# State-space scan with a feed-forward layer on one core: the written-out issue order of the first four units re-sorted

## The chip, the cores and the metric

The kernel runs on one core of one Trainium2 chip. The metric is the device time of the kernel in microseconds (us). Lower is better.

## The reference

The reference computes a chunked state-space scan, and feeds its result into a two-layer network with a squared ReLU. Cut to what matters:

```
# x [4,8,768,32], a [4,8,768], B and C [4,8,768,16]; chunk = 32 positions
for c in range(768 // 32):
    cum   = cumsum(log(clip(a_c, 1e-6, 1)))
    M     = (C_c @ B_c.T) * exp(cum_i - cum_j) * causal      # per batch and head
    y_c   = M @ x_c + (C_c @ state) * exp(cum_i)
    state = exp(sum(la)) * state + sum_j B_j x_j exp(cum_last - cum_j)
t   = y.transpose(0, 2, 1, 3).reshape(3072, 256)
out = (maximum(t @ w_in, 0) ** 2) @ w_out                    # 256 -> 2048 -> 256
```

## The kernel before

**Units.** The 3072 tokens are cut into 12 units of 256 tokens: one of four batches, one of three thirds of the sequence. The first thirds of the four batches come first, so that the scan's state reaches a unit four units later. The scan works on a whole unit at once. The products P of the decays are folded into C, and their inverses (`Pinv`) into x, so that what is left of M is a plain product C·B under a 0/1 mask.

**Steps of a unit k.** Each step is a short word in a list, with the unit's number behind it.
- `ldC`, `ldB`, `ldx`: loads of float32 C, B, x, issued on SP's queue. `pc` (`prep_c`, L167): C scaled by P into a bf16 tile `jt`, in two instructions. `pb` (`prep_b`, L175 or L179): B cast into `jt`. `px` (`prep_x`, L187): x scaled by `Pinv`, into `xs`.
- `tr`: `jt` turned around into `bct`. For units 0 to 3 TensorE does it (L205), and `tc` copies the result out (L218 on ScalarE, L220 on VectorE); from unit 4 on a transposing transfer of SP's queue does it (L196).
- `mt`: the 16 score matmuls C·B (L235) into PSUM banks 0 to 3. `mk`: VectorE masks one bank straight from PSUM (L244). Instead of that, `sc` copies a bank to SBUF on ScalarE (L249), and `ms` masks the copy (L253) on VectorE or GpSimd.
- `u`: the state's update (L260, 16 matmuls, `xs` by `jt`). `ina`, `inb`: the two halves of the masked scores times `xs` (L260, 32 matmuls together). `sf`: the first state scaled (L388, tile `Sd`). `ca`: C times the state (L260, 2 matmuls `bct` by `Sd`). `t`: the unit's result copied into `T` (L218, L220, L327). `us`, `za`, `sa` and the like carry the state on.
- `a0` to `a7` for unit 0, `b0` to `b7` for unit 1 and so on: one eighth of the first layer, 4 matmuls of `w_in_b` (L451) and a ReLU on ScalarE (L472). `qa0`: VectorE squares it (L478). `A0` to `A7`: one eighth of the second layer (4 matmuls, L451 again), accumulated in one bank; the last one is followed by a copy to `osb` (L500) and the store (L501).
- `id`: filler matmuls on constants (L552). `wi0` to `wi3`, `wo0` to `wo3`: the four pieces of w_in and w_out, issued by GpSimd (L148, L152).
- `gB3` and the like: a small memset (L143) that keeps a load back until the engine named gets to it. `afC`, `afK`, `afS`: small copies on GpSimd (L668 to L676) that hold GpSimd's following work back until a C, a prefix scan or a state is there.
- `ac1`, `p2`, `pp1`, `pd`, `iv`: decay products of the second and last third. `p2` is 16 matmuls (L519, L523, L632); the last four of them need `pick_p`, which `pp1` makes on ScalarE (L620). `pd` copies the result, and `iv` makes `Pinv` of it. `jz2` (L593) clears the third `jt` tile.

**What sets the order.** Nothing is planned at run time. One string `ORDER` is split at blanks, and each word issues its step; each engine works off its own instructions in that order, and waits on semaphores. `:a`, `:v`, `:p`, `:s` behind a word name the engine or queue (ScalarE, VectorE, GpSimd, SP), `:va` one for each of two instructions, `@3` a PSUM bank.

Of the kernel before, what the change touches and what calls it, by code (L numbers as in the profile page):

```python
# [30 lines left out]
def kernel(  # L31
# [14 lines left out]
    NH, S, D, N = 8, 768, 32, 16  # L46
    NU = 12
    ORDER = """
        fa1:a jz0:v ef jz1:p id3:512 ti fa0:s la0:s id4:512 pi eb ldB0:s ac0:v ldC0:a sk0 ku sp la1:a pbh0:p hd id1:256
        pc0:v pbl0:v mb:a id2:512 trC0 ps iv:8:16 tcC0:1:a tcC0:0:v trB0 la2:s tcB0:2:v pk id1:512 iv1:0:8 id1:512  # L50
        ldx0:s mt0 wi0 la3:s px0:v ldC1:s su id2:512 ldB1:s wi1 ldx1:s u0:67 mk0 fq mk0 gC2:v mk0 ac1:v pc1:p sc0 pb1:a
        id2:512 tr1 id4:512 tc1:1:a tc1:0:a to ms0:p sf0 sk1 wo0 afK px1:p wi2 mt1 ina0 inb0 ca0 pp1:a mk1 mk1 t0:aa sc1
        us0 mk1 fr p2@4 a0 ldC2:s a1 u1::6 ina1 ms1:v wo1 wi3 jz2:p pc2 inb1 sf1 ca1 pd t1:va us1 a3@0 qa1 ldB2:s qa0
        a2@1 wo2 b0@2 qa3 qb0 b1@3 qb1 b2@4 b3@5 A0 A1 B0 pb2:p B1 tr2 zb0 qb3 gB3:v ldx2:s ldB3:s ldC3:s ldx3:s b4 a4
        iv:32:64 zb1 tc2:1:v qa2 tc2:0:v b5 sb1 sb0 qb4 a5 qb2 qa4 mt2 sc2 B3 iv:16:32 px2 pc3 wo3 mk2 mk2 sc2 A3 A2
        ms2:v ms2:v qa5 a6 b6 pb3:a B2 a7 qb5 qa6 b7 u2 ina2 inb2 sf2 afS2 px3 ld4 A4 tr3 ca2 tc3:1:v t2:aa B4 us2 B5
        tc3:0:v u3:45 pc4 mt3 A5 us3 sc3 c5 qb7 qb6 mk3 za3 pb4 ldC5:s ldB5:s c3 qa7 c4 qc5 c0 qc3 px4 tr4 ldx5:s pb5
        pc5 sa3 c1 c6 ldC6:s tr5 ldB6:s ldx6:s qc4 qc0 A6 px5 pq A7 wm c2 B6 c7 C0 ms3:v mk3 qc6 mk3 qc7 afC2 pc6 B7 C3
        C6 C4 qc1 bk rg4 C1 qc2 d1 d0 za4 sa4 pb6 mk4 mk4 d3 mk4 C5 d4 qd0 d2 mk4 px6 tr6 ld7 C2 C7 qd1 qd2 qd3 zb3 rg5
        sb3 D0 mk5 za5 sa5 D1 mk5 d5 qd4 D2 pc7 pb7 d6 qd5 d7 qd6 D3 zb2 e0 qd7 mk5 e1 qe0 sb2 D4 mk5 D5 tr7 ld8 e2 qe1  # L60
        D6 e3 qe2 ml px7 rg6 e4 D7 qe3 za6 sa6 zb6 mk6 e5 qe4 sb6 e6 qe5 e7 qe6 iv:64:96 mk6 E0 E1 E2 E3 ldC9:s ldB9:s
        px8 mk6 f0 qe7 E4 f1 qf0 pc8 E5 pb8 tr8 ldx9:s E6 mk6 f2 qf1 f3 qf2 E7 rg7 mk7 F0 f4 qf3 za7 F1 F2 f5 qf4 f6 qf5
        f7 qf6 g0 qf7 zb7 sa7 sb7 mk7 F3 mk7 F4 pc9 pb9 tr9 px9 ld10 g1 qg0 F5 mk7 g2 qg1 zb4 sb4 F6 g3 qg2 F7 rg8 za8
        zb8 sa8 sb8 g4 qg3 G0 mk8 g5 qg4 G1 mk8 g6 qg5 G2 g7 qg6 G3 mk8 h0 qg7 G4 pc10 pb10 tr10 px10 ld11 h1 qh0 G5 mk8
        zb5 sb5 h2 qh1 G6 h3 qh2 G7 rg9 za9 zb9 sa9 sb9 h4 qh3 H0 mk9 h5 qh4 H1 mk9 h6 qh5 H2 h7 qh6 H3 mk9 i0 qh7 H4
        pc11 pb11 tr11 px11 i1 qi0 H5 mk9 i2 qi1 H6 i3 qi2 H7 rg10 za10 zb10 sa10 sb10 i4 qi3 I0 mk10 i5 qi4 I1 mk10 i6
        qi5 I2 i7 qi6 I3 mk10 j0 qi7 I4 j1 qj0 I5 mk10 j2 qj1 I6 j3 qj2 I7 rg11 za11 zb11 sa11 sb11 j4 qj3 J0 mk11 j5
        qj4 J1 mk11 j6 qj5 J2 j7 qj6 J3 mk11 k0 qj7 J4 k1 qk0 J5 mk11 k2 qk1 J6 k3 qk2 J7 rg12 k4 qk3 K0 k5 qk4 K1 k6
        qk5 K2 k7 qk6 K3 l0 qk7 K4 l1 ql0 K5 l2 ql1 K6 l3 ql2 K7 l4 ql3 L0 l5 ql4 L1 l6 ql5 L2 l7 ql6 L3 ql7"""
    LATE = 6  # L70
    WIN = [(0, 2), (2, 4), (4, 6), (6, 8)]
    WOUT = [(0, 2), (2, 4), (4, 6), (6, 8)]
# [807 lines left out]
```

## Time and profile before

| | |
|---|---|
| times of three runs | 113.91, 113.81, 113.87 us; median 113.87 us |
| the profiled execution | 113.92 us, with a span of 112.2 us and 3692 instructions |
| mean granted TensorE clock | 1.0 |
| TensorE busy | 106.8 us (95%) in 1453 matmuls |
| VectorE, ScalarE, GpSimd busy | 83.0, 76.8, 50.9 us |
| moved by DMA | 13.44 MB, 120 GB/s on average |

The span runs from the first to the last instruction of the profiled execution; 1.72 us of its time lie around it. The times named in the text are microseconds from the start of the span. In a row of the timeline the first number is the start and the second the time from the first to the end of the last of the instructions put together there; the bracket behind it is the idle time before it and what ended it.

### The profile page before, as it was taken

How to read it: one execution, taken by the hardware profiler on the slowest of the kernel's cores; microseconds unless marked ns; L12 is line 12 of the kernel's file. 1: busy time of each engine (PE TensorE's matmuls, PEld its weight loads, DVE VectorE, ACT ScalarE, POOL GpSimd, SP SyncE). 2: the span in 40 equal slices, each digit the busy share in tenths (PEclk: the TensorE clock that was granted, in tenths of full speed). 3: DMA queues.
4: the chain of work that ended last, by engine and by line, in shares of the span. 5: the costliest groups of instructions: out<-in, count | busy, mean ns of one | idle time of the engine just before them, and what ended most of it. 6: DMA issues, size and time to landing. Idle time of an engine off the chain costs nothing.

```text
span 112.2 us, 3692 instructions
## 1 busy us (share of the span) xinstructions
PE 106.8 (95%) x1453; PEld 92.0 (82%) x1454; DVE 83.0 (74%) x189; ACT 76.8 (68%) x159; POOL 50.9 (45%) x98
## 2 busy tenths in 40 slices
PE   6988999998999999999999999999999999999990
PEld 2434799886997989989989989889899899899980
DVE  1688858996793988979977989679589398355440
ACT  1745994885894776685677676877876867867840
POOL 7589973259676564378038653573160020000000
PEclk9999999999999999999999999999999999999999
DMA  1999999979989799987994997799680020020203
GB/s 38 198 186 164 211 193 201 156 148 188 148 171 97 92 284 64 110 188 72 103 179 48 138 217 74 99 196 98 129 211 0 6 96 0 29 70 0 93 0 94
DMA packets 67281, 13.44 MB, mean 120 GB/s; under 512 B 63104, under 2 KB 65984, under 8 KB 67264
## 3 DMA queue, kind: packets, MB, share of 16 engines
q1 hardware_dynamic: 64320, 10.88, 59.3%
q0 software_dynamic: 1664, 2.10, 11.4%
q10 hardware_dynamic: 1280, 0.23, 1.1%
q8 instruction: 11, 0.18, 0.7%
q14 instruction: 6, 0.05, 0.1%
HBM read 10.58 MB, written 3.15 MB: 122 GB/s over the span
## 4 chain that ended last, share of the span: by engine, by line
PE 77%; DMA 8%; ACT 4%; SPq 3%; POOL 2%; issue 2%; DVE 1%; ACTq 0%; POOLq 0%
PE pp L451 66%; PE pp L260 6%; DMA C_nat<-in_C_dram 5%; DMA B_nat<-in_B_dram 3%; ACT hb L472 2%; PE pp L229 2%; SPq L134 1%; SPq L654 1%; PE pp L235 1%; POOL jt L167 1%; POOL xs L187 1%; ACT bct L218 1%; PE pp L205 0%; DVE Sd L388 0%; DVE h L478 0%
## 5 line engine op out<-in xcount | busy, mean ns | idle before, releaser
L472 ACT ACTIVATE hb<-pp 128x512 bf16<-128x512 f32 x96 | 54.5, 602 | 21.8 <-PE pp L451 20.2
L451 PE MATMUL pp<-w_out_b,h 128*128 128x256 bf16 (+1 forms) x400 | 53.8, 268 | 0.0
L451 PE MATMUL pp<-T,w_in_b 128*128 128x256 bf16 x384 | 53.3, 273 | 0.0
L478 DVE TENSOR_TENSOR h<-hb 128x512 bf16<-128x512 bf16 x96 | 44.5, 485 | 11.4 <-ACT hb L472 11.2
L451 PEld LDWEIGHTS <-w_in_b 128*128 128x128 bf16 x384 | 41.4, 114 | 1.8 <-issue 1.1
L451 PEld LDWEIGHTS <-h 128*128 128x128 bf16 x400 | 37.6, 98 | 4.5 <-issue 1.0
L244 DVE TENSOR_TENSOR mts<-pp,mask 128x512 bf16<-128x512 f32 x43 | 28.5, 678 | 1.3 <-PE pp L235 0.7
L187 POOL TENSOR_TENSOR xs<-x_nat,Pinv 128x256 bf16<-128x256 f32 (+1 forms) x19 | 13.4, 722 | 14.8 <-DMA x_nat<-in_x_dram 6.7
L376 POOL TENSOR_TENSOR Sd<-z,Pquad 128x256 bf16<-128x256 f32 x16 | 11.0, 698 | 10.0 <-DVE z L360 6.7
L167 POOL TENSOR_TENSOR jt<-C_nat,P_sb 128x128 bf16<-128x128 f32 x22 | 10.0, 472 | 8.9 <-DMA C_nat<-in_C_dram 8.8
L360 DVE SCALAR_TENSOR_TENSOR z<-z,Ptot,us 128x64 f32<-128x64 f32 x8 | 3.3, 407 | 7.4 <-ACT us L344 5.0
L552 PE MATMUL pp<-const-bfloat16-1.0 128*128 128x512 bf16 (+1 forms) x19 | 6.5, 464 | 1.0 <-PEq L864 0.8
L500 ACT COPY osb<-pp 128x512 f32<-128x512 f32 x11 | 6.4, 583 | 0.4 <-PE pp L451 0.4
L175 POOL CAST jt<-B_nat 128x256 bf16<-128x256 f32 x9 | 4.6, 511 | 3.9 <-DMA B_nat<-in_B_dram 2.9
L260 PE MATMUL pp<-mts,xs 64*32 64x128 bf16 (+1 forms) x288 | 5.4, 219 | 0.0
L260 PE MATMUL pp<-bct,Sd 128*128 128x128 bf16 x40 | 4.2, 220 | 0.2 <-DVE Sd L388 0.2
L552 PEld LDWEIGHTS <-const-bfloat16-1.0 128*128 128x128 bf16 x20 | 1.8, 111 | 2.6 <-issue 2.2
L260 PEld LDWEIGHTS <-xs 64*32 64x32 bf16 (+1 forms) x288 | 3.6, 93 | 0.4 <-issue 0.2
L260 PEld LDWEIGHTS <-Sd 128*128 128x128 bf16 x40 | 3.0, 98 | 0.7 <-DVE Sd L388 0.4
L260 PEld LDWEIGHTS <-jt 64*32 64x32 bf16 (+1 forms) x128 | 1.6, 90 | 2.2 <-issue 1.2
L249 ACT CAST sc<-pp 128x512 bf16<-128x512 f32 x5 | 2.9, 607 | 0.6 <-PE pp L235 0.5
L148 POOL DMA_DIRECT2D w_in_b<-in_moe_w_in_dram x4 | 3.1, 776 | 0.3 <-issue 0.3
(77 smaller groups left out, 58.3 us busy)
## 6 DMA issues: line engine op xcount, KB each, us to landing
out_dram<-osb SPq DMA_DIRECT2D x11, 256.0 KB, 3.0
x_nat<-in_x_dram SPq DMA_DIRECT2D x6, 256.0 KB, 4.9
w_in_b<-in_moe_w_in_dram POOLq DMA_DIRECT2D x4, 256.0 KB, 5.6
w_out_b<-in_moe_w_out_dram POOLq DMA_DIRECT2D x4, 256.0 KB, 6.4
B_nat<-in_B_dram SPq DMA_DIRECT2D x6, 128.0 KB, 4.5
C_nat<-in_C_dram SPq DMA_DIRECT2D x12, 64.0 KB, 3.9
B_nat<-in_B_dram SPq DMA_DIRECT2D x12, 64.0 KB, 3.0
x_nat<-in_x_dram SPq DMA_DIRECT2D x6, 128.0 KB, 3.3
```

The costliest lines, as they stand in the source:

```text
L167: eng.tensor_tensor(out=_fap(jt[k % 3], 128 + 144 * g, [[384, 2], [32, 4], [1, 16]]), in0=_fap(loaded[k]["C"], 128 * g, [[16, 2], [32, 4], ...
L175: fn(out=_fap(jt[k % 3], 0, [[384, 2], [16, 2], [32, 4], [1, 16]]), in_=_fap(loaded[k]["B"], 0, [[16, 2], [128, 2], [32, 4], [1, 16]]))
L187: eng.tensor_tensor(out=_fap(xs, 256 * r, [[256, 2 // n], [32, 8], [1, 32]]), in0=_fap(loaded[k]["x"], 32 * r, [[32, 2 // n], [64, 8], [1, ...
L244: nc.vector.tensor_tensor(out=live[k]["mts"][:, q].rearrange("p r g i -> p (r g i)"), in0=pp[:, q, :], in1=mask1 if k >= LATE else mask, o ...
L260: nc.tensor.matmul(dst, w, v, start=bool(need), stop=False, skip_group_check=True, **({} if pos is None else {"tile_position": pos}))
L360: nc.vector.scalar_tensor_tensor(out=z, in0=prev[0], scalar=Ptot[:, total(1, b, j - 1):total(1, b, j - 1) + 1], in1=us, op0=ALU.mult, op1= ...
L376: nc.gpsimd.tensor_tensor(out=_fap(S_d, 0, [[128, 2], [32, 4], [1, 32]]), in0=_fap(z, 0, [[32, 2], [0, 4], [1, 32]]), in1=_fap(Pquad, 4 * ...
L451: nc.tensor.matmul(dst, w(0, 128), v, skip_group_check=True, **flags)
L472: nc.scalar.activation(out=hb.rearrange("p i t -> p (i t)"), in_=pp[:, h, :], func=AF.Relu)
L478: nc.vector.tensor_tensor(out=h2, in0=hb, in1=hb, op=ALU.mult)
L500: nc.scalar.copy(out=osb, in_=pp[:, 6 if blk == 1 else 7, :])
L552: nc.tensor.matmul(pp[:, h, 0:int(cols)], ones_b[:, 0:128], ones_b[:, 0:int(cols)] if dep is None else dep, start=True, stop=True, skip_gr ...
```

## The change

The first 234 of the list's 561 words are re-sorted; the 327 from `bk rg4 C1` on, which is the fifth unit's feed-forward work and everything behind it, stay as they are. No function is changed. The parts:

- Engines: `px0` goes from VectorE to GpSimd and stands behind `pc1`; `pbl0` and a copy of unit 0's turned C go from VectorE to ScalarE; one copy of `tc1` from ScalarE to VectorE; `jz2` from GpSimd to VectorE; both halves of `t1` onto VectorE; `pb2` from GpSimd and `pb3` from ScalarE to VectorE. Of unit 2 one ScalarE copy with its mask (`sc2`, `ms2`) becomes a direct mask (`mk2`).
- Start: `u0`, `ina0` and `inb0` stand around unit 1's transposes and scores; `pp1` stands behind `t0`, not ahead of it; one more filler stands ahead of `ca1`, others are moved. 20 filler matmuls there are in both.
- Weights: the fourth piece of w_in (`wi3`) is issued behind `pc2`, which was the other way round.
- Middle: `B3` stands ahead of `mt2`, `b5` behind `B2`, `mt3` ahead of `u3`.
- Loads: B of unit 5 stands ahead of its C; C of unit 6 and x of unit 5 stand ahead of the two transposing transfers of units 4 and 5; B and x of unit 6 stand behind the first store.

```
-  … ldx0:s mt0 wi0 la3:s px0:v ldC1:s su … wi1 ldx1:s u0:67 mk0 fq mk0 gC2:v mk0 ac1:v pc1:p sc0 pb1:a id2:512 tr1
-  id4:512 tc1:1:a tc1:0:a to ms0:p sf0 sk1 wo0 afK px1:p wi2 mt1 ina0 inb0 ca0 pp1:a mk1 mk1 t0:aa sc1
-  us0 mk1 fr p2@4 a0 ldC2:s a1 u1::6 ina1 ms1:v wo1 wi3 jz2:p pc2 inb1 sf1 ca1 pd t1:va us1 a3@0 …
-  b3@5 A0 A1 B0 pb2:p B1 tr2 zb0 qb3 gB3:v ldx2:s ldB3:s ldC3:s ldx3:s b4 a4 … b5 … mt2 sc2 B3 … A3 A2 …
-  … A4 tr3 ca2 tc3:1:v t2:aa B4 us2 B5 tc3:0:v u3:45 pc4 mt3 A5 …
-  ldC5:s ldB5:s … tr4 ldx5:s pb5 pc5 sa3 c1 c6 ldC6:s tr5 ldB6:s ldx6:s qc4 …
+  … ldx0:s iv1:0:8 wi0 mt0 la3:s ldC1:s su … ldx1:s sc0 mk0 wi1 mk0 pc1:p pb1:a px0:p fq id4:512 ms0:p tr1@01 tc1:1:a
+  mk0 gC2:v u0:67:5 ina0 tc1:0:v to id1:512 mt1 sf0 inb0 ac1:v wo0 sk1 afK ca0 px1:p t0:aa pp1:a mk1 mk1 wi2
+  mk1 us0 fr sc1 p2@4 a0@0 a1@1 ms1:v wo1 u1::6 sf1 pd ldC2:s ina1 inb1 jz2:v pc2 wi3 id1:512 ca1 t1:vv us1 a3@0 …
+  b3@5 b2 qb1 A0 ldx2:s A1 B0 B1 zb0 qb3 pb2:v tr2 gB3:v ldB3:s ldC3:s ldx3:s b4 … B3 mt2 mk2 … A3 … A2 … b5 …
+  ldB5:s qa6 ca2 B5 tc3:1:v t2:aa B4 us2 pb4 tc3:0:v mt3 u3:45 us3 ldC5:s … ldC6:s ldx5:s … tr4 … tr5 …
+  … C0 ldB6:s ldx6:s C3 …
```

In the rows below a tile's name has its unit and a running number at the end; all lines of the changed file are 20 lower, since the string is shorter (L147 is L167 of the profile, and so on).

On GpSimd, from the scaling of C for unit 1 to that for unit 2, before:

```order
L167 TENSOR_TENSOR jt1_111<-C_nat1_207,P_sb_106 128x2x4x16 x2
L253 TENSOR_TENSOR mts0_202<-sc0_3_242,mask_90 128x512
L152 DMA w_out_b0_117<-in_moe_w_out_dram 128x1024
L672 COPY gate_cp_266<-cp128_103 128x1
L187 TENSOR_TENSOR xs1_268<-x_nat1_215,Pinv_107 128x512
L148 DMA w_in_b2_115<-in_moe_w_in_dram 128x2x512
L152 DMA w_out_b1_118<-in_moe_w_out_dram 128x1024
L148 DMA w_in_b3_116<-in_moe_w_in_dram 128x2x512
L593 MEMSET jt2_112 128x768
L167 TENSOR_TENSOR jt2_112<-C_nat2_236,P_sb_106 128x2x4x16 x2
```

The same stretch of GpSimd after:

```order
L147 TENSOR_TENSOR jt1_111<-C_nat1_205,P_sb_106 128x2x4x16 x2
L167 TENSOR_TENSOR xs0_222<-x_nat0_183,Pinv_107 128x512
L233 TENSOR_TENSOR mts0_203<-sc0_0_214,mask_90 128x512
L132 DMA w_out_b0_117<-in_moe_w_out_dram 128x1024
L652 COPY gate_cp_314<-cp128_103 128x1
L167 TENSOR_TENSOR xs1_318<-x_nat1_212,Pinv_107 128x512
L128 DMA w_in_b2_115<-in_moe_w_in_dram 128x2x512
L132 DMA w_out_b1_118<-in_moe_w_out_dram 128x1024
L147 TENSOR_TENSOR jt2_112<-C_nat2_239,P_sb_106 128x2x4x16 x2
L128 DMA w_in_b3_116<-in_moe_w_in_dram 128x2x512
```

The scaling of unit 0's x has come in ahead of the mask of its score copy, the clearing of the third `jt` tile has gone, and the fourth piece of w_in is issued behind unit 2's C.

On ScalarE, from the cast of unit 1's B to the first ReLU, before:

```order
L175 CAST jt1_111<-B_nat1_212 128x2x2x4x16
L218 COPY bct1_247<-pp_121 128x384 x2
L609 COPY Ptot_108<-pp_121 128x8
L620 ACTIVATE pick_p128_105<-pick_95,cp128_103 128x16
L218 CAST T0_325<-pp_121 128x4x64 x2
L249 CAST sc1_2_328<-pp_121 128x512
L341 COPY us0_330<-pp_121 128x128
L472 ACTIVATE hb0_0_345<-pp_121 128x512
```

The same stretch of ScalarE after:

```order
L155 CAST jt1_111<-B_nat1_210 128x2x2x4x16
L198 COPY bct1_230<-pp_121 128x384
L589 COPY Ptot_108<-pp_121 128x8
L198 CAST T0_320<-pp_121 128x4x64 x2
L600 ACTIVATE pick_p128_105<-pick_95,cp128_103 128x16
L324 COPY us0_328<-pp_121 128x64 x2
L229 CAST sc1_3_331<-pp_121 128x512
L452 ACTIVATE hb0_0_345<-pp_121 128x512
```

The activation that makes `pick_p` now follows the two copies of unit 0's result, and one of the two copies of unit 1's transposes is gone to VectorE.

On SP's queue, from the x of unit 4 to the first store, before:

```order
L134 DMA x_nat4_683<-in_x_dram 128x8x64
L134 DMA C_nat5_768<-in_C_dram 128x8x32
L134 DMA B_nat5_770<-in_B_dram 128x8x32
L196 DMA_TRANSPOSE bct4_799<-jt1_111 128x6x128
L134 DMA x_nat5_801<-in_x_dram 128x8x64
L129 DMA C_nat6_820<-in_C_dram 128x8x16 x2
L196 DMA_TRANSPOSE bct5_823<-jt2_112 128x6x128
L129 DMA B_nat6_825<-in_B_dram 128x8x16 x2
L129 DMA x_nat6_828<-in_x_dram 128x8x32 x2
L501 DMA out_0_dram<-osb0_847 128x512
```

The same stretch of SP after:

```order
L114 DMA x_nat4_676<-in_x_dram 128x8x64
L114 DMA B_nat5_693<-in_B_dram 128x8x32
L114 DMA C_nat5_750<-in_C_dram 128x8x32
L109 DMA C_nat6_760<-in_C_dram 128x8x16 x2
L114 DMA x_nat5_763<-in_x_dram 128x8x64
L176 DMA_TRANSPOSE bct4_790<-jt1_111 128x6x128
L176 DMA_TRANSPOSE bct5_825<-jt2_112 128x6x128
L481 DMA out_0_dram<-osb0_846 128x512
L109 DMA B_nat6_865<-in_B_dram 128x8x16 x2
L109 DMA x_nat6_868<-in_x_dram 128x8x32 x2
```

The transposing transfer of unit 4 has three loads ahead of it that stood behind it, and the first store overtakes four loads.

More of the change, by code (lines that the diff above doesn't have):

```diff
@@ L48 @@
     ORDER = """
[L49 to L68, printed above, removed]
@@ L69 @@
-        qk5 K2 k7 qk6 K3 l0 qk7 K4 l1 ql0 K5 l2 ql1 K6 l3 ql2 K7 l4 ql3 L0 l5 ql4 L1 l6 ql5 L2 l7 ql6 L3 ql7"""
+        jz0:v jz1:p fa1:a ef id3:512 fa0:s ac0:v ti pi la0:s id4:512 eb ldB0:s ku ldC0:a sk0 sp la1:a mb:a id1:512 pbh0:p pc0:v id2:512 trC0 ps iv:8:16 hd pbl0:a tcC0:1:a tcC0:0:a la2:s trB0 tcB0:2:v pk id1:512 id1:512 ldx0:s iv1:0:8 wi0 mt0 la3:s ldC1:s su id2:512 ldB1:s ldx1:s sc0 mk0 wi1 mk0 pc1:p pb1:a px0:p fq id4:512 ms0:p tr1@01 tc1:1:a mk0 gC2:v u0:67:5 ina0 tc1:0:v to id1:512 mt1 sf0 inb0 ac1:v wo0 sk1 afK ca0 px1:p t0:aa pp1:a mk1 mk1 wi2 mk1 us0 fr sc1 p2@4 a0@0 a1@1 ms1:v wo1 u1::6 sf1 pd ldC2:s ina1 inb1 jz2:v pc2 wi3 id1:512 ca1 t1:vv us1 a3@0 qa0 a2@1 ldB2:s b0@2 wo2 qa3 b1@3 qa1 qb0 b3@5 b2 qb1 A0 ldx2:s A1 B0 B1 zb0 qb3 pb2:v tr2 gB3:v ldB3:s ldC3:s ldx3:s b4 iv:32:64 zb1 tc2:1:v qb2 tc2:0:v sb1 qa2 a4 qb4 a5 qa4 sb0 B3 mt2 mk2 iv:16:32 px2:p pc3:p sc2 ms2:v wo3 mk2 mk2 qa5 A3 pb3:v A2 a6 b6@1 B2 b5 qb5 a7 b7@3 u2 ina2 inb2 sf2 ld4 afS2 px3:p A4 tr3 ldB5:s qa6 ca2 B5 tc3:1:v t2:aa B4 us2 pb4 tc3:0:v mt3 u3:45 us3 ldC5:s sc3 A5 pc4 ldC6:s ldx5:s c5 qb6 za3 qa7 mk3 c4 qb7 c3 tr4 qc5 px4 c0 pb5 qc3 pc5 c1 pq sa3 qc0 c6 tr5 qc4 c7 px5 A6 A7 c2 B6 afC2 C0 ldB6:s ldx6:s C3 ms3:v mk3 qc6 mk3 wm qc7 C4 qc1 pc6 C6 B7 bk rg4 C1 qc2 d1 d0 za4 sa4 pb6 mk4 mk4 d3 mk4 C5 d4 qd0 d2 mk4 px6 tr6 ld7 C2 C7 qd1 qd2 qd3 zb3 rg5 sb3 D0 mk5 za5 sa5 D1 mk5 d5 qd4 D2 pc7 pb7 d6 qd5 d7 qd6 D3 zb2 e0 qd7 mk5 e1 qe0 sb2 D4 mk5 D5 tr7 ld8 e2 qe1 D6 e3 qe2 ml px7 rg6 e4 D7 qe3 za6 sa6 zb6 mk6 e5 qe4 sb6 e6 qe5 e7 qe6 iv:64:96 mk6 E0 E1 E2 E3 ldC9:s ldB9:s px8 mk6 f0 qe7 E4 f1 qf0 pc8 E5 pb8 tr8 ldx9:s E6 mk6 f2 qf1 f3 qf2 E7 rg7 mk7 F0 f4 qf3 za7 F1 F2 f5 qf4 f6 qf5 f7 qf6 g0 qf7 zb7 sa7 sb7 mk7 F3 mk7 F4 pc9 pb9 tr9 px9 ld10 g1 qg0 F5 mk7 g2 qg1 zb4 sb4 F6 g3 qg2 F7 rg8 za8 zb8 sa8 sb8 g4 qg3 G0 mk8 g5 qg4 G1 mk8 g6 qg5 G2 g7 qg6 G3 mk8 h0 qg7 G4 pc10 pb10 tr10 px10 ld11 h1 qh0 G5 mk8 zb5 sb5 h2 qh1 G6 h3 qh2 G7 rg9 za9 zb9 sa9 sb9 h4 qh3 H0 mk9 h5 qh4 H1 mk9 h6 qh5 H2 h7 qh6 H3 mk9 i0 qh7 H4 pc11 pb11 tr11 px11 i1 qi0 H5 mk9 i2 qi1 H6 i3 qi2 H7 rg10 za10 zb10 sa10 sb10 i4 qi3 I0 mk10 i5 qi4 I1 mk10 i6 qi5 I2 i7 qi6 I3 mk10 j0 qi7 I4 j1 qj0 I5 mk10 j2 qj1 I6 j3 qj2 I7 rg11 za11 zb11 sa11 sb11 j4 qj3 J0 mk11 j5 qj4 J1 mk11 j6 qj5 J2 j7 qj6 J3 mk11 k0 qj7 J4 k1 qk0 J5 mk11 k2 qk1 J6 k3 qk2 J7 rg12 k4 qk3 K0 k5 qk4 K1 k6 qk5 K2 k7 qk6 K3 l0 qk7 K4 l1 ql0 K5 l2 ql1 K6 l3 ql2 K7 l4 ql3 L0 l5 ql4 L1 l6 ql5 L2 l7 ql6 L3 ql7"""
```

## Prediction

> **What bounds the kernel now.** I read the busy times first, then the chain of waits, then the busy time by stretches, and the timeline where these point.
>
> ```profile
> span 112.2 us, 3692 instructions
> PE 106.8 (95%) x1453; PEld 92.0 (82%) x1454; DVE 83.0 (74%) x189; ACT 76.8 (68%) x159; POOL 50.9 (45%) x98
> ```
>
> ```profile
> 0.00:13.75 13.75, 11.67 (x197) 5.93 (x199) 9.28 (x26) 7.74 (x20) 11.15 (x28) 1.00 1.00 159
> 13.75:26.76 13.01, 13.01 (x180) 11.63 (x179) 10.24 (x28) 9.97 (x23) 7.24 (x13) 1.00 1.01 174
> 26.76:27.40 0.64, 0.28 (x24) 0.25 (x32) 0.64 (x3) 0.00 (x0) 0.64 (x2) 1.00 1.21 216
> 27.40:109.30 81.90, 81.89 (x1062) 74.21 (x1062) 62.84 (x136) 58.81 (x115) 31.82 (x58) 1.00 0.65 105
> ```
>
> In the second block the columns are the stretch, its length, and busy time and count of TensorE, its weight loads, VectorE, ScalarE and GpSimd, then granted clock, DMA share and GB/s. TensorE is full from 13.75 to 26.76 and from 27.40 to the end at 109.30; both kernels have the same feed-forward matmuls in there. So the time can change in three ways only: the full stretch starts at another time, the one gap at 27 us goes, or a new gap opens. The chain of waits, in order of time, says what makes the gap:
>
> ```profile
> 18.43 5.69 DMA C_nat<-in_C_dram
> 24.26 1.06 POOL jt L167 x2
> 25.32 0.35 POOL w_out_b L152
> 26.08 1.00 POOL xs L187
> 27.12 0.25 PE pp L260 x16
> ```
>
> C of unit 3 lands at 24.12, GpSimd scales it, issues a weight piece, scales x3, and only then may TensorE do u3. Everything else in 13.75 to 109.30 hides behind TensorE, and so do all steps in the change that I don't price below: the casts, masks and copies that change engines there start 0.5 us or more ahead of their users, by VectorE's 10.24 and ScalarE's 9.97 busy of 13.01 in that stretch. The 20 fillers run in waits that stay. The tail of the list is the same.
>
> The profiled execution took 113.92, 0.05 over the median of 113.87, with 1.72 around its span; I sum against 113.92 and take the 0.05 off at the end. Within 0.2%, or 0.23 us, a measurement of this kernel can't tell from no change.
>
> **The start.** The rows, as they run into the first feed-forward matmuls:
>
> ```profile
> 7.55 0.76 POOL L167 TENSOR_TENSOR jt<-C_nat,P_sb 128x128 bf16<-128x128 f32 x2 [0.30 <-DMA C_nat<-in_C_dram]
> 8.27 1.14 POOL L253 TENSOR_TENSOR mts<-sc,mask 128x512 bf16<-128x512 bf16 x1
> 10.16 0.42 PE L235 MATMUL pp<-bct 32*64 32x256 bf16 x16
> 10.20 0.31 ACT L620 ACTIVATE pick_p<-pick,cp 128x16 f32<-128x16 f32 x1
> 10.38 1.04 POOL L187 TENSOR_TENSOR xs<-x_nat,Pinv 128x512 bf16<-128x512 f32 x1
> 10.51 0.46 PE L260 MATMUL pp<-mts,xs 64*32 64x128 bf16 x32
> 11.09 0.65 ACT L218 CAST T<-pp 128x256 bf16<-128x256 f32 x2 [0.58 <-PE pp L260]
> 11.58 0.24 PE L632 MATMUL pp<-pick_p,spread 128*64 128x16 f32 x4
> 11.78 1.03 PE L451 MATMUL pp<-T,w_in_b 128*128 128x256 bf16 x8
> 12.75 0.25 PE L260 MATMUL pp<-xs,jt 64*32 64x64 bf16 x16
> 13.15 0.42 DVE L388 TENSOR_TENSOR Sd<-pp,Pquad 128x256 bf16<-128x256 f32 x1 [0.30 <-PE pp L260]
> 13.63 0.29 PE L260 MATMUL pp<-bct,Sd 128*128 128x128 bf16 x2 [0.24 <-DVE Sd L388]
> ```
>
> x0 moves onto GpSimd behind C1. That C lands at 7.55, so GpSimd now does C1 (0.76, to 8.31), x0 (1.04, to 9.35) and the mask (1.14, to 10.49). The second half of unit 0's masked scores needs that mask; before, the whole block stood at 10.51. So it comes at 10.5 as it did, though the scores of unit 1, which no longer stand in the way, come 0.4 earlier. The first copies of T0 started 0.58 behind the block's first matmul, with 32 matmuls and the carry to do; now 16 of the 32 are done, which at 0.46 for 32 is some 0.2 less: the copies start at 10.9 and end at 11.55. ScalarE then makes `pick_p` (0.31) where before it had made it at 10.20, ahead of the copies: ready at 11.86; successive records of one engine overlap by some hundredths (GpSimd's at 7.55 lasts 0.76, and the next begins at 8.27), so I take 11.81. The last four matmuls of `p2` (L632) stand ahead of a0 in TensorE's queue and wait for it. They start at 11.81 against 11.58, and a0, 0.20 behind, at 12.02 against 11.78: **+0.24**. Behind `p2` nothing shrinks: u1, the first state (0.42) and its carry follow one on the other, each waiting, so that the carry at 13.63 comes at 13.87 and the full stretch begins at 13.99. The filler added ahead of the carry lies in that wait. If the start were covered instead, this term would be 0 or below it; by the 0.4 that unit 1's scores gain, −0.4 is its lower end, and +0.3 (the whole of `pick_p`) its upper.
>
> **B of unit 2.** Its cast goes from GpSimd to VectorE, behind the square of the fifth ReLU.
>
> ```profile
> 4.96 0.23 DVE L179 CAST jt<-B_nat 128x128 bf16<-128x128 f32 x1
> 15.75 0.41 POOL L175 CAST jt<-B_nat 128x256 bf16<-128x256 f32 x1
> 17.54 0.43 DVE L478 TENSOR_TENSOR h<-hb 128x512 bf16<-128x512 bf16 x1 [0.36 <-ACT hb L472]
> 18.12 0.50 PE L205 MATMUL pp<-eye_b,jt 128*128 128x128 bf16 x6
> ```
>
> It was done 2 us ahead of the transposes at 18.12. The square ends at 17.97, one half of such a cast takes VectorE 0.23, so the whole between 0.23 and 0.46; I take 0.36, and the transposes may start at about 18.40. Their place, shifted by the start's 0.24, is 18.36: **+0.04**, with −0 and +0.15 as ends.
>
> **The gap.** TensorE was at u3's place long before it could begin:
>
> ```profile
> 27.12 0.25 PE L260 MATMUL pp<-xs,jt 64*32 64x64 bf16 x16 [0.37 <-POOL xs L187]
> 26.68 0.09 PEld L260 LDWEIGHTS <-jt 64*32 64x32 bf16 x1 [0.21 <-ACT us L341]
> 26.29 0.62 DVE L220 COPY bct<-pp 128x384 bf16<-128x384 bf16 x2 [0.95 <-PE pp L260]
> ```
>
> The second row is the weight load of u3's first matmul, at 26.68; the matmul followed 0.44 later, where a weight load and its matmul else start within 0.1 of each other. Without the wait u3 would have stood at 26.68. In the list `mt3` now stands ahead of it: 16 score matmuls (0.42 in the row at 10.16, the tail of the last one counted) fill the wait. They need `bct3`, whose last copy ended at 26.91 (the third row), and unit 2's masked banks, which are free. u3 then comes at 26.68 + 0.28 from the two terms above + 0.36, about 27.32, and x3 is there at 27.12 if C3 comes when it did. The gap is covered with 0.2 to spare: **−0.44**, and **+0.03** for one more change of shape. What is late next is nothing that TensorE waits for. Ends: 0 (the wait persists) and −0.44.
>
> **The sum:** +0.24 + 0.04 − 0.44 + 0.03 = −0.13; 113.79 against the profiled execution, 113.74 against the median. I give 113.75, which a measurement would call the same.
>
> **The rivals.**
>
> *The start is not late (faster, 113.55).* If GpSimd is done with the mask a third of a microsecond sooner, or `pick_p` doesn't stand at the end of ScalarE's line, the full stretch starts where it did or up to 0.4 sooner. The gain is then bounded by x3 at 27.12: u3 can't come sooner, but `mt3` is already done, which is worth its 0.36, less 0.03: 113.92 − 0.33 − 0.05 = 113.54. For it: the scores of unit 1 do come sooner, and VectorE is relieved of x0. Against it: the order on ScalarE is fixed, and C1's landing holds GpSimd.
>
> *The third unit's loads come later (same, 113.9).* The memset that lets B3, C3 and x3 go stands behind the cast of B2 on VectorE, 0.3 later. If the landing moves with it, x3 is ready at 27.44, 0.1 behind u3's place, and each 0.1 more costs 0.1; with 0.25 more the result is 113.9. Against it: C3 took 5.69 from its issue, so its queue set its landing and not its issue.
>
> *The fourth w_in piece is late (slower, 114.3).* It was issued at 12.68. Now GpSimd first does C of unit 2, which waits for VectorE's clearing of `jt2`, and issues the piece at about 15.1.
>
> ```profile
> 12.68 0.70 POOL L148 DMA_DIRECT2D w_in_b<-in_moe_w_in_dram  x1
> 14.23 0.97 POOL L167 TENSOR_TENSOR jt<-C_nat,P_sb 128x128 bf16<-128x128 f32 x2
> DMA to landing us min/median/max: 4.6/5.6/7.9
> 21.97 1.04 PE L451 MATMUL pp<-T,w_in_b 128*128 128x256 bf16 x8
> ```
>
> The third row is the landing time of the four pieces. a6 and b6 (last row) are the first to need it, at 21.97 + 0.28 − 0.44 (b5 now stands behind them) = 21.81. It lands at 20.7 by the median and 23.0 by the slowest. From 6.7 us of landing time on TensorE stands, by 1.2 at the slowest; half of that gives 113.75 + 0.6 = 114.35. Against it: the slowest piece was queued behind other weights.
>
> *The fourth unit's transposing transfer is late (slower, 114.3).* SP issued it at 28.61, ahead of x5 and C6; now behind.
>
> ```profile
> 28.61 2.39 SPq L196 DMA_TRANSPOSE bct<-jt  x1
> 31.67 1.59 SPq L129 DMA_DIRECT2D C_nat<-in_C_dram  x2
> DMA to landing us min/median/max: 2.8/3.4/5.3
> 35.81 0.42 PE L235 MATMUL pp<-bct 32*64 32x256 bf16 x16
> ```
>
> The three loads hold the queue for 1.59 + 0.56 (x5, alone) up to some 5 us when they are held themselves, so that it goes out between 30.3 and 33.5, and lands 3.4 later by the median (third row), at 33.7 to 36.9. The scores of unit 4 want it at 35.81 − 0.13 = 35.68. Half of the worst 1.2 is 0.6: 114.3. It decides once the transfer goes out behind 32.3.
>
> *A lock between VectorE and GpSimd (slower, 114.05).* Unit 2's x on GpSimd and the mask of the score copies on VectorE now start together at about 22.0.
>
> ```profile
> 22.02 1.05 POOL L187 TENSOR_TENSOR xs<-x_nat,Pinv 128x512 bf16<-128x512 f32 x1 [2.03 <-DMA x_nat<-in_x_dram]
> 22.27 1.42 DVE L253 TENSOR_TENSOR mts<-sc,mask 128x512 bf16<-128x512 bf16 x2
> ```
>
> Two such masks took 1.42 here; the first began inside GpSimd's x2 and by its own row lasted until that ended. If x2 is first again, the masks are some 0.65 late, b7's bank is freed late, and TensorE stands up to 0.3: 113.75 + 0.3 = 114.05. The Trainium skill ("SBUF — State Buffer", section "Who interferes with whom") says that the port pair which VectorE shares with GpSimd is the one source of contention, and an exclusive lock; the 1.42 for two masks agrees. By that rule x0 on GpSimd could be blocked too wherever VectorE works on two SBUF operands in 8.3 to 10.5, which would make the start later yet; VectorE's work there reads PSUM for the most part, and so I price nothing.
>
> **How the numbers follow.** The forecast has .40, with a range of its own from 113.6 to 113.97 by the ends of its small terms. A start that isn't late has .30, late loads .10, the weight piece .07, the transfer .07, the lock .06. Faster is the second case and .03 of the first, .33; slower the last three, .20; the same the rest, .47. The range reaches from 113.4 (the second case with x3 0.15 sooner) to 114.3.
>
> **What would show it.** In the profile after: `pick_p` behind T0's copies and a0 at about 12.0; the full stretch from 14.0; transposes of unit 2 at 18.4; `mt3` ahead of u3 and no wait for `xs` at u3; a6 without a wait for w_in, unit 4's scores without one for `bct`. The prediction is wrong if a0 comes at 11.8 or before, if the wait at u3 stays, or if a gap opens near 21.8, 23 or 35.7.

## The result, and the profile after

The changed kernel takes 115.5 us (median of 6 runs, 114.58 to 116.24), the one before 113.89 (113.81 to 115.01) beside it: a ratio of 1.0116, with a 95% interval from 1.0075 to 1.0157. It is slower here, and its times lie far apart. In two later comparisons, on two chips, its median was 114.77 beside 114.58 and 115.57 beside 114.28. The ratios given here leave out executions more than 1.5% above the fastest of their kernel (eight of twelve in the first experiment below); medians and spreads are over all.

The profiled execution took 114.74, near the lower end. The page's first lines, and the busy time by stretches, cut where TensorE stands (columns as before):

```profile
span 113.0 us, 3692 instructions
PE 107.4 (95%) x1452; PEld 92.6 (82%) x1454; DVE 83.7 (74%) x191; ACT 75.8 (67%) x158; POOL 51.0 (45%) x97
```

```profile
0.00:13.84 13.84, 12.08 (x197) 6.57 (x200) 8.70 (x24) 7.69 (x23) 11.17 (x27) 1.00 0.98 157
13.84:18.54 4.70, 4.70 (x48) 4.48 (x46) 3.97 (x14) 3.33 (x9) 2.29 (x4) 1.00 0.96 160
18.54:19.60 1.06, 0.17 (x3) 0.00 (x1) 0.97 (x5) 0.00 (x0) 0.86 (x2) 1.00 1.16 182
19.60:110.08 90.48, 90.47 (x1210) 81.51 (x1210) 70.10 (x153) 64.55 (x127) 36.65 (x65) 1.00 0.68 111
```

The gap at 27 us has gone, as forecast: TensorE is full from 19.60 to 110.08. A new one stands from 18.54 to 19.60. The chain of waits, in order of time, leads to it:

```profile
8.17 1.00 POOL xs L167
9.18 1.11 POOL mts L233
10.29 0.56 POOL w_out_b L132
10.85 0.06 issue
10.90 0.18 POOL gate_cp L652
11.09 0.96 POOL xs L167
12.05 7.50 DMA w_in_b<-in_moe_w_in_dram
19.56 0.05 issue
19.60 1.94 PE pp L431 x16
```

x0 and the mask hold GpSimd from 8.17 to 10.29. The first w_out piece, the scaling of x1 and then the third w_in piece go out behind them. That piece is issued at 12.05 and lands 7.5 later. Before, it was issued at 11.37 and landed 5.1 later:

```profile
11.37 0.76 POOL L148 DMA_DIRECT2D w_in_b<-in_moe_w_in_dram  x1
DMA to landing us min/median/max: 5.1/5.1/5.1
```

The fifth eighths of both units (b4, a4) want the piece at 18.54. The wait is in the table of waits:

```profile
PE pp L431 <- DMA w_in_b<-in_moe_w_in_dram: 0.9, 1, 0.9
```

The end of the feed-forward work moved from 109.31 to 110.08, +0.77: the start +0.09, this stall +1.06, the gap −0.44, the rest +0.06. That accounts for this execution, but not for those of 115.4 and more.

### The profile page after: what moved, and what is told of

Its sections match the earlier page's. It is cut to its first block, busy times and chain, and to the rows that moved or that the text cites. A ratio compares the mean times of both kernels' runs of the same rounds, so it can differ in the third digit from the quotient of the medians.

```text
span 113.0 us, 3692 instructions
## 1 busy us (share of the span) xinstructions
PE 107.4 (95%) x1452; PEld 92.6 (82%) x1454; DVE 83.7 (74%) x191; ACT 75.8 (67%) x158; POOL 51.0 (45%) x97
## 4 chain that ended last, share of the span: by engine, by line
PE 84%; DMA 7%; POOL 4%; ACT 1%; issue 1%; DVE 0%; ACTq 0%
PE pp L431 71%; DMA w_in_b<-in_moe_w_in_dram 7%; PE pp L240 6%; PE pp L532 3%; PE pp L209 2%; POOL xs L167 2%; PE pp L215 2%; POOL mts L233 1%; PE pp L185 1%; ACT sc L229 1%; POOL w_out_b L132 0%; PE pp L509 0%; DVE jt L147 0%; POOL jt L147 0%; ACT osl L818 0%
## 5 line engine op out<-in xcount | busy, mean ns | idle before, releaser
L224 DVE TENSOR_TENSOR mts<-pp,mask 128x512 bf16<-128x512 f32 x44 | 29.2, 679 | 1.2 <-PE pp L209 0.6
L167 POOL TENSOR_TENSOR xs<-x_nat,Pinv 128x256 bf16<-128x256 f32 (+1 forms) x20 | 14.9, 759 | 14.9 <-PE pp L209 5.1
L356 POOL TENSOR_TENSOR Sd<-z,Pquad 128x256 bf16<-128x256 f32 x16 | 10.8, 688 | 10.5 <-DVE z L340 7.1
L147 POOL TENSOR_TENSOR jt<-C_nat,P_sb 128x128 bf16<-128x128 f32 x22 | 9.6, 456 | 9.5 <-DMA C_nat<-in_C_dram 8.7
L340 DVE SCALAR_TENSOR_TENSOR z<-z,Ptot,us 128x64 f32<-128x64 f32 x8 | 4.0, 495 | 6.6 <-ACT us L324 5.4
L532 PE MATMUL pp<-const-bfloat16-1.0 128*128 128x512 bf16 x18 | 6.2, 477 | 0.8 <-PEq L844 0.8
L240 PE MATMUL pp<-xs,jt 64*32 64x64 bf16 (+1 forms) x128 | 2.9, 196 | 0.1
```

The source lines that it names most:

```text
L147: eng.tensor_tensor(out=_fap(jt[k % 3], 128 + 144 * g, [[384, 2], [32, 4], [1, 16]]), in0=_fap(loaded[k]["C"], 128 * g, [[16, 2], [32, 4], ...
L167: eng.tensor_tensor(out=_fap(xs, 256 * r, [[256, 2 // n], [32, 8], [1, 32]]), in0=_fap(loaded[k]["x"], 32 * r, [[32, 2 // n], [64, 8], [1, ...
L224: nc.vector.tensor_tensor(out=live[k]["mts"][:, q].rearrange("p r g i -> p (r g i)"), in0=pp[:, q, :], in1=mask1 if k >= LATE else mask, o ...
L240: nc.tensor.matmul(dst, w, v, start=bool(need), stop=False, skip_group_check=True, **({} if pos is None else {"tile_position": pos}))
L340: nc.vector.scalar_tensor_tensor(out=z, in0=prev[0], scalar=Ptot[:, total(1, b, j - 1):total(1, b, j - 1) + 1], in1=us, op0=ALU.mult, op1= ...
L356: nc.gpsimd.tensor_tensor(out=_fap(S_d, 0, [[128, 2], [32, 4], [1, 32]]), in0=_fap(z, 0, [[32, 2], [0, 4], [1, 32]]), in1=_fap(Pquad, 4 * ...
```

## The experiments

"Mended version" below is the changed kernel with four words of the list moved (two loads and two weight pieces), as the third of the second group shows.

### First group: which piece, and why it is late

The third w_in piece sooner:

```
- wo0 sk1 afK ca0 px1:p … mk1 mk1 wi2 mk1
+ wo0 wi2 sk1 afK ca0 px1:p … mk1 mk1 mk1
```

> The changed kernel with the third w_in piece issued right behind the first w_out piece, 1.2 us earlier (10.85 instead of 12.05), ahead of the scaling of x1. Theory A (the third piece is late because its issue slipped on GpSimd behind x0 and the mask): it lands by about 17, the 1.06 us that TensorE stands at 18.5 goes, and the time is 114.74 - 1.06 = 113.7 in the profiled execution; if the fourth piece, issued at 15.2, is then late as well, 113.9. Theory B (the third piece is slow because the fourth one's issue moved behind C of unit 2, and the weight queue runs thin): still over 114.5. Theory C (the loads on SP's queue collide with it, whenever it is issued): 114.3 to 114.7.

Median 116.91 (113.87 to 118.41) beside 114.5; ratio 1.002 [0.9966, 1.0075]. The profiled one took 118.41, has no wait for a weight piece in the full stretch, and stands elsewhere: TensorE's scores of unit 4 (`mt4`), in the timeline:

```profile
32.40 3.42 SPq L176 DMA_TRANSPOSE bct<-jt  x2
38.62 0.42 PE L215 MATMUL pp<-bct 32*64 32x256 bf16 x16 [2.50 <-DMA bct<-jt]
```

The transposing transfer of unit 4, the first of the two issues from 32.40, landed 6.2 later. By theory A the kernel should have got faster; only two of its twelve executions (113.87 and 114.34) lie below the median beside it. In the profiled one the first wait is out of the way and the second shows in full. What came behind it adds to the price. The rows give TensorE's busy time by stretches, then the granted clock, DMA share and GB/s:

```profile
38.60:39.60 1.00, 0.98 (x22) 1.00 1.15 282
39.60:40.60 1.00, 1.00 (x8) 0.61 0.73 69
40.60:41.60 1.00, 1.00 (x7) 0.50 1.07 155
41.60:42.60 1.00, 1.00 (x6) 0.50 1.16 242
42.60:43.60 1.00, 1.00 (x9) 0.69 0.42 149
```

One microsecond after the wait the clock falls to a half for some 3 us, in which 6 to 9 matmuls run per us, where 12 run in the next one at a clock of 1.00. In the whole execution it was 0.985.

The fourth piece in its old place:

```
- jz2:v pc2 wi3 id1:512 ca1
+ wi3 jz2:v pc2 id1:512 ca1
```

> The changed kernel with the fourth w_in piece ahead of the scaling of unit 2's C, as before the change (issue at 13.4 instead of 15.2). Theory A (late issue of the third piece): the third piece lands at 19.5 as in the changed kernel, TensorE stands about 1 us at 18.5, time 114.7. Theory B (the weight queue runs thin because of the fourth piece's place): the third piece lands by 18 and the time is 113.7. Theory C (collision with SP's loads): as A.

Median 115.86 (114.3 to 118.53) beside 114.5; ratio 1.0071 [1.0032, 1.011]. The third piece, issued at 12.19, landed at 17.29: no stall at 18.5, as theory B has it. The fourth landed 9.0 after its issue, at 22.50, and held TensorE for 0.5; and `mt4` waited 2.2 for its transfer. So B was right on the third piece and the time didn't follow.

The slip alone, in the kernel before:

```
- afK px1:p wi2 mt1 … wo1 wi3 jz2:p pc2
+ afK px1:p jz2:p wi2 mt1 … wo1 wi3 pc2
```

> The kernel before, with GpSimd's clearing of jt2 (0.77) moved ahead of the third w_in piece's issue, so that this goes out at 12.14 instead of 11.37, and the fourth piece at 13.45; nothing else of the change is in it. Theory A: the third piece lands at 18.8 to 19.6 and TensorE stands 0.4 to 1.2 us at 18.5: 114.3 to 115.1. Theory B: it lands by 17.5, as the queue behind it is full: 113.9. Theory C (the collision comes from what the change moved elsewhere): 113.9.

Median 114.81 (113.77 to 115.24) beside 114.5; ratio 1.0018 [0.9986, 1.0051]. Issued at 12.20, the third piece landed at 18.10, in time. The slip alone did not make it late in this profile, as theory A would have it.

The scores of unit 3 ahead of its state update, in the kernel before:

```
- u3:45 pc4 mt3 A5
+ mt3 u3:45 pc4 A5
```

> The kernel before, with the score matmuls of unit 3 ahead of its state update and nothing else of the change. By the prediction's working the wait of 0.44 at 27.1 us is covered: -0.36 to -0.44 with +0.03 for one more change of shape, 113.45 to 113.55. Rival: the wait moves to the next matmul that needs a result of the state update, and the time stays at 113.85.

Median 114.82 (113.79 to 116.61) beside 114.5; ratio 1.0002 [0.9966, 1.0038]. No gain is seen, though the interval just reaches the forecast. In the profile TensorE's wait moved by one place:

```profile
26.64 0.62 DVE L220 COPY bct<-pp 128x384 bf16<-128x384 bf16 x2 [0.95 <-PE pp L260]
27.31 0.42 PE L235 MATMUL pp<-bct 32*64 32x256 bf16 x16 [0.21 <-DVE bct L220]
```

The scores wait for the copies of `bct3`, and only 0.15 of the 0.64 between the last matmul ahead and the first behind is saved (0.49 here).

### Second group: the transfer

> The changed kernel once more, beside the next three. Two landings cost it: the third w_in piece at 18.5 us (1.06 in its first profile) and, in executions that are slower than that one, unit 4's transposing transfer at about 36 us (2.5 us in two relatives of it). Theory D (two landings, both decided by how long a transfer takes): +0.7 to +2.5 against the kernel before, with a spread over 1 us, and a wait for one or both in the profile. Theory E (one landing only, w_in): +0.7 to +1.0, with no wait at 36 us.

Median 114.77 (113.81 to 115.65) beside 114.58; ratio 1.0003 [0.9959, 1.0046]. The profiled execution (114.66) waits 0.5 in all for w_in, none for the transfer. On this chip the whole change cost nothing, beyond what the interval leaves.

The transfer ahead again:

```
- pc4 ldC6:s ldx5:s c5 … c3 tr4 qc5
+ pc4 c5 … c3 tr4 ldx5:s ldC6:s qc5
```

> The changed kernel with the transposing transfer of unit 4 ahead of x of unit 5 and C of unit 6 on SP's queue, as before the change. Theory D: the wait at 36 us goes in all executions, the one at 18.5 us stays: +0.5 to +1.0 against the kernel before, with half the spread of the changed kernel. Theory E: as the changed kernel.

Median 114.62 (114.03 to 115.72); ratio 1.0016 [0.9985, 1.0047]. The profiled one, the slowest at 115.72, has no wait at 36 us, 0.8 of weight loads' wait for w_in (the third piece landed at 18.88, the fourth at 22.54), and 0.9 for a later unit's transfer, at 66.5. With w_in late this mend is worth nothing that the intervals show.

Both landings mended (that edit, and the two of the first group's `wi2` and `wi3`):

> The changed kernel with that transfer ahead, with the third w_in piece issued right behind the first w_out piece, and the fourth ahead of unit 2's C. Theory D: no wait for a landing is left; the start comes up to 0.5 later, since x1 now stands behind the issue of the third piece on GpSimd, the wait at u3 is covered (-0.44): -0.4 to +0.2 against the kernel before. If over +0.5, a third cause is in the change.

Median 113.94 (113.72 to 114.81) beside 114.58; ratio 0.9963 [0.9931, 0.9995]. The full stretch starts at 14.08, and no gap is left. Its places at u3 and `mt4`:

```profile
27.02 0.42 PE L215 MATMUL pp<-bct 32*64 32x256 bf16 x16
27.37 0.25 PE L240 MATMUL pp<-xs,jt 64*32 64x64 bf16 x16
28.89 2.13 SPq L176 DMA_TRANSPOSE bct<-jt  x1
35.75 0.42 PE L215 MATMUL pp<-bct 32*64 32x256 bf16 x16
```

The same edit of the transfer, the other way round, in the kernel before:

```
- px4 tr4 ldx5:s pb5 … c6 ldC6:s tr5
+ px4 ldC6:s ldx5:s tr4 pb5 … c6 tr5
```

> The kernel before with that one part of the change: the transposing transfer of unit 4 behind C of unit 6 and x of unit 5. Theory D: the transfer goes out at 31 to 33 instead of 28.6, and TensorE waits up to 2.5 us at 35.8 in part of the executions: median +0.5 to +2.0, with a spread over 1 us. Rival (the queue behind is late only together with the later w_in piece): 0.

Median 115.47 (115.14 to 116.72) beside 114.58; ratio 1.0107 [1.0056, 1.0158]. This one move costs by itself as much as the whole change in the first comparison. On this same chip the whole change cost nothing that shows, so there the move cost less, or other parts saved as much; which of the two is not shown. Its profile:

```profile
28.25 3.10 SPq L129 DMA_DIRECT2D C_nat<-in_C_dram  x2
31.39 0.57 SPq L134 DMA_DIRECT2D x_nat<-in_x_dram  x1
32.14 3.89 SPq L196 DMA_TRANSPOSE bct<-jt  x2
37.31 0.42 PE L235 MATMUL pp<-bct 32*64 32x256 bf16 x16 [1.24 <-DMA bct<-jt]
```

C of unit 6 takes 3.10 to get out where it took 1.59 before, the transfer goes at 32.14 instead of 28.61, and lands at 37.2 where 36.1 was wanted.

### Third group: the two terms of the sum

The mended version with u3 ahead of `mt3` again (`mt3 u3:45` becomes `u3:45 mt3`):

> The version with both landings mended (the transposing transfer ahead, third and fourth w_in piece issued sooner), with the state update of unit 3 ahead of its scores again, as before the change. Theory F (the wait of 0.44 at u3 goes because the scores fill it, the prediction's term): +0.36 to +0.44 against the mended version. Theory G (the later start has eaten the wait already, since x3's time is set by the landing of C3 and not by TensorE: x3 is there at 27.06, u3's place would be 27.0): 0 to +0.15.

Median 114.12 (113.81 to 115.51) beside 114.28; ratio 0.9996 [0.9965, 1.0026]. u3 came 0.28 after the start of the matmul ahead of it, where the scores in its place come 0.20 after it and find their copies long done: 0.08 lost, not 0.44. Theory G holds by the profile; on the time the intervals of this and the next overlap.

`pick_p` ahead of T0's copies (`t0:aa pp1:a` becomes `pp1:a t0:aa`):

> The mended version with pick_p made ahead of the two copies of T0 on ScalarE, as before the change. If the prediction's term for the start is right, a0 and the full stretch begin 0.2 to 0.3 sooner (12.15 and 14.08 in the mended version). Theory G: the end comes only 0 to 0.1 sooner, because the scores of unit 3 then wait for the copies of its transposes and u3 for x3. Theory F: the whole 0.2 to 0.3.

Median 113.98 (113.62 to 114.89) beside 114.28; ratio 0.9979 [0.9951, 1.0008]. The last matmuls of `p2` come at 11.57 against 11.93 in the mended version, so `pick_p` did hold them. The first w_in piece then holds a0 for 0.2, so that a0 comes at 12.03 against 12.15 and the full stretch at 13.96 against 14.08 and 14.13 in its two sisters. The profiled execution later waits 0.4 for another unit's transfer.

The fourth piece late, in the kernel before (`wi3 jz2:p pc2` becomes `jz2:p pc2 wi3`):

> The kernel before with one part of the change: the fourth w_in piece issued behind the scaling of unit 2's C (15.2 instead of 12.7). Theory B (with a gap in the weight issues x2's load gets the engines, and all later pieces land later): x2 lands at 19.8 to 21.4 instead of 21.9 to 23.5; the fourth piece lands at 22.0 to 22.5, where a6 wants it at 22.0: +0.1 to +0.6. Theory A (only the slip behind x0 on GpSimd counts): 0.

Median 114.12 (113.56 to 115.05) beside 114.28; ratio 0.9987 [0.9959, 1.0016]. x2 lands at 19.52, 2.4 sooner than in the first profile of before. Both weight pieces are in time (17.33 and 21.07). By itself this part costs nothing that the interval shows.

> The changed kernel a third time, for a profile of another execution and the spread of its times beside the kernel before. Theory D (two landings, w_in at 18.5 to 22.5 us and the transposing transfer at 36.5): waits for w_in of 0.3 to 1.1 and, where these are small, a wait for the transfer of up to 2.5, since what is waited for at 18 to 22 needs not be waited for again at 36; +0.2 to +2.0. Theory E: waits for w_in alone.

Median 115.57 (114.24 to 119.15) beside 114.28; ratio 1.0067 [1.0033, 1.0101]. The profiled execution (114.90) waits 0.5 for the third w_in piece, to 19.35, and 0.1 for the second w_out piece, which lands at 20.92; it does not wait at 36 us. The slowest of the twelve, 119.15, had a mean clock of 0.985, the same as the two executions of the first group that waited 2.2 and 2.5 for the transfer; it has no profile.

### Single executions of the changed kernel

None of its three profiles so far is of an execution over 115.4.

> The changed kernel, one execution with its profile. Theory D: if it takes over 115.4, TensorE waits over 0.5 us for the transposing transfer at 36 us, and its waits for w_in are no more than 1.1; if it takes 114.2 to 115.0, the waits for w_in alone make it up. Theory E: the waits for w_in make up the excess at any time.

113.71: no wait for a landing at all. From the start of the full stretch to the end there is no gap:

```profile
13.92:109.08 95.16, 95.14 (x1259) 85.97 (x1256) 75.90 (x168) 67.83 (x136) 40.20 (x70) 1.00 0.69 116
```

> As the look before: over 115.4 with a wait of over 0.5 us at 36 us by theory D, without one by theory E.

115.35: the third w_in piece landed at 17.07, in time, and the transfer, issued at 31.32, 5.8 later. The chain of waits and then the table of waits:

```profile
31.32 5.82 DMA bct<-jt
37.15 0.04 issue
37.19 0.42 PE pp L215 x16
```

```profile
PE pp L215 <- DMA bct<-jt: 1.4, 1, 1.4
```

> As the look before: over 115.4 with a wait of over 0.5 us at 36 us by theory D, without one by theory E.

114.18: 0.3 of weight loads' wait for the fourth w_in piece, which landed at 22.07, and nothing else.

> As the look before: over 115.4 with a wait of over 0.5 us at 36 us by theory D, without one by theory E.

114.97: 0.5 for w_in in two places, 0.2 for the transfer. None of the four took over 115.4, so the bound written down was not put to the test. But the slowest of them, by 0.4, is the one with the long wait for the transfer, as theory D has it; and 118.41 and 118.53 of the first group's two variants show the same wait at 2.5 and 2.2. What an execution of the changed kernel over 115.4 waits for is not shown.

## Why the prediction was wrong

It gave 113.75 with 113.4 to 114.3, and put both late landings, a w_in piece and the transfer, outside its sum, at 0.14 together. Point by point:

- **The sum** was for an execution in which all landings are in time. One such took 113.71, where the sum said 113.74; but the kernel before took 114.30 beside it, so the agreement is in part luck. The noise was set too low as well: against 0.23 us, the kernel before spread over 1.2 us in the six runs beside the result.
- **The start, +0.24.** In the first profile after it was +0.09, with a0 at 11.91. Over the seven profiled executions of the changed kernel the full stretch starts at 13.84 to 14.15, on average at 14.03: +0.28 against 13.75. The path was as foretold, and a_T4_w_pp1 shows that `pick_p` sets it: `pick_p` (L600) behind the copies of T0, the last matmuls of `p2` (L612) behind it, a0 last.

```profile
10.78 0.65 ACT L198 CAST T<-pp 128x256 bf16<-128x256 f32 x2 [1.11 <-PE pp L240]
11.31 0.32 ACT L600 ACTIVATE pick_p<-pick,cp 128x16 f32<-128x16 f32 x1
11.68 0.29 PE L612 MATMUL pp<-pick_p,spread 128*64 128x16 f32 x4
11.91 1.06 PE L431 MATMUL pp<-T,w_in_b 128*128 128x256 bf16 x8
```

- **B of unit 2, +0.04.** The cast took 0.29, and the transposes came at 18.21, in their shifted place. 0. The working's own 18.40 does not follow from its parts: 17.97 and 0.36 make 18.33.
- **The gap, −0.44.** It went, but for the most part not through `mt3`. A start that is 0.28 later uses up most of a wait whose end is set by the landing of C3; with u3 in its old place 0.08 was left to gain, and in the kernel before the swap saved 0.15 in the profile. In b_wi3late, where TensorE came there 0.8 later for other reasons, u3 had no wait without the swap. So start and gap may stand in one sum, but neither is worth its figure alone: without the swap the wait at 27 us takes up the whole 0.24 lost at the start.
- **One more change of shape, +0.03.** No row stands behind this term, and it measured 0: from the first of the two groups to the matmul behind them it is 0.54 in either order (27.02 to 27.56 in a_T4_w, 27.15 to 27.69 in a_T4_w_u3).
- **The weight piece** was priced as a rival, with one of two pieces. I followed the fourth, whose place had changed in the list: it came as bounded (landing at 21.06 to 22.77), and weight loads waited 0.3 to 0.4 for it in three of the seven profiles. I did not follow the third, which was left in its place but stands behind x0 and the mask on the same queue. The step that failed is "x0 moves onto GpSimd": it counted 1.04 for the mask that follows, and stopped there. The first w_out piece, x1 and the third w_in piece come 0.7 to 0.9 later with it. That slip is the smaller part: of the 3.1 by which the third piece's landing moved in the first profile, 0.7 is the issue and 2.4 a longer transfer.

The landing of the third piece, by what was changed (times of issue and landing from the profiles; it is wanted at 18.5 to 18.8):

| | fourth piece ahead of C of unit 2 | fourth piece behind it |
|---|---|---|
| third issued at 10.8 to 11.5 | 16.47 (before) to 17.73, six profiles | 17.33 (b_wi3late), 17.68 (a_wi2_early) |
| third issued at 12.1 to 12.3 | 17.29 (a_wi3_early), 18.10 (b_jz2_first) | 17.07 to 19.55, median 18.98 (seven of the changed kernel); 18.88 (a_T4) |

Landings of the third piece that made TensorE or its weight loads wait are in the lower right alone: five of eight, from 18.88 on. One part without the other gave none, but four profiles are few beside five of eight, so that it takes both parts is likely and not shown.

What lengthens the transfer there stays open. The transfer engines are full in this stage in both kernels (share 0.96 and more), and the load of x2 runs beside the pieces, on the other queue. But its landing doesn't tell: 21.94 in the profile of before, 19.79 to 24.08 in the four executions of the changed kernel with the third piece late, and 19.46 to 22.48 in the three with it in time. So it isn't seen that x2 gets what the weights lose. The Trainium skill ("DMA: Bandwidth & Descriptors", section "SWDGE vs HWDGE vs iDMA") says that each transfer engine takes the queues of GpSimd and of SP in turn. No run here shows what that makes of these two loads.

- **The transfer** was a rival with 0.07. Its issue was rightly bounded (30.3 to 33.5; 31.3 to 32.8 was seen). The landing was mis-sized: I took 3.4, the median over all eight transfers, most of which run where the transfer engines have little else to do (the share is 0.45 from 60 to 109 us, and 1.00 from 28.5 to 36). In this stage the profile of before already had 3.9 for this transfer and 4.6 for the next, the ends of its line on the two from 28 to 34 us:

```profile
DMA to landing us min/median/max: 3.9/4.2/4.6
```

  And the landing, not only the issue, goes with the place in the queue. With the loads behind the transfer it took 2.8 to 3.9 in eight profiles; with them ahead 3.7 to 6.2 in ten, of which the four that waited over 1 us had 5.1 to 6.2. The changed kernel's own seven had 3.7 to 4.0, and 5.8 once. With 3.9 and the middle of the issue's bounds the working gives 31.9 + 3.9 = 35.8 against 35.68 wanted: no slack is left, and with 5.8 it gives a stall of 2.0. The rival should have been part of the forecast. Alone the move gave a ratio of 1.0107 (b_T4late). Why four landings took so long is not shown.
- **Two late landings don't add.** One at 18.5 shifts TensorE's need of the next by as much. The changed kernel's profiles show a long wait for one or the other, never both; with the first mended alone the second cost 2.5 in the one profile there is. Both mended, it was slightly faster than before on one chip (0.9963 [0.9931, 0.9995]); two near relatives on another (0.9996 and 0.9979) have intervals that reach past 1. What the executions of 115.5 and more in the first comparison waited for is not shown; the transfer is the likeliest by the above.
- **The lock** cost TensorE nothing: in the first profile it has no gap in 22.8 to 24.1. In the profile of before, where x2 began first (22.02), the first mask took 1.08 and ended at 23.35, 0.28 behind x2, where the kernel's other masks of that shape on VectorE took 0.42. In the profile after, the mask began first (22.81, x2 at 22.97) and took 0.36, and x2 1.10. On GpSimd x0 and the mask behind it took 1.00 and 1.11, no more than the 1.04 and 1.14 that the working counted.

## What to carry to other kernels

When an instruction moves onto an engine that also issues transfers, follow every transfer behind it on that queue to its landing and to the instruction that needs it, also those whose place in the code is unchanged. Price a landing from the same stage of the profile and with its longest case, never from a median over the whole run, and where that leaves less than 1 us of slack, forecast a spread and not a point. A wait whose end is set by a transfer takes up any delay ahead of it, so a term on either side of it is not worth its figure alone, and mending one of two late transfers may gain nothing.

## What the runs showed of the hardware

A wait of 2.5 us on TensorE had an aftermath: the granted clock stayed at 1.00 for 1 us, then fell to 0.5, and was back at 1.00 some 5 us after the wait (rows above); a wait of 2.2 (a_wi3_early) was followed by 0.57, 0.50, 0.50 and 0.72 in the four microseconds from 40 us, and a wait of 1.4 (a_look2) left it at 1.00 throughout. The Trainium skill ("TensorE: Matmul & The Clock Gate", section "What's actually happening") puts the fall at an idle window of some 3.4 us. Here 2.5 and 2.2 were enough.

The same program also differed between comparisons: the kernel before had a median of 113.89 beside the first result, and of 114.50, 114.58 and 114.28 on the three chips of the later groups. Three of its four profiled relatives there have a gap on TensorE behind the 23rd matmul of the full stretch (0.25 in b_mt3, 0.31 in b_jz2_first, 0.50 in b_wi3late) that the first profile of before doesn't have, nor any profile of the changed kernel or its variants. If the kernel before itself has it there, the later ratios flatter the change. The chain of waits in b_mt3 names nothing that was waited for:

```profile
13.82 2.51 PE pp L451 x23
16.33 0.25 issue
16.58 2.05 PE pp L451 x17
```

What this is stays open.
